# The first loads, the order of the queues, and two sums in the logits' banks: one change to a transformer block on one core

## The chip, the core and the metric

The kernel runs on one core of a Trainium2 chip. TensorE (PE) does the matmuls, VectorE (DVE), ScalarE (ACT) and GpSimd (POOL) the rest; SyncE (SP) issues nearly all DMAs. The metric is device time in microseconds (us); lower is better.

## The reference

One block on x of 2048 x 512 (bfloat16): a layernorm with scale and shift, sliding dilated attention (32 heads of 16, 8 keys at steps of 2) with a gated residual, a second such layernorm, and a gated FFN of width 1792 with a gated residual. Scales, shifts and gates are six blocks of 512 from one vector.

```python
mod = (silu(c) @ w_mod).reshape(c.shape[0], 6, 1, -1)
sa, ca, ga, sb, cb, gb = mod[:, 0..5]
h = layernorm(x) * (1 + ca) + sa
qkv = h @ wqkv                               # 32 heads of 16
idx = pos[:, None] - 2 * arange(8)           # masked where negative
logits = einsum('bhsd,bhswd->bhsw', q, k[idx]) * scale
x = x + ga * (einsum('bhsw,bhswd->bhsd', softmax(logits), v[idx]) @ wo)
h = layernorm(x) * (1 + cb) + sb
x = x + gb * ((gelu(h @ w_gate) * (h @ w_up)) @ w_down)
```

## The kernel before, in words

The 2048 rows go in four groups (0 to 3) of 512. For each group: layernorm statistics (`norm`, on DVE; `norm_act`, on ACT for some chunks), the normalised xn, a transpose, scale and shift into hT, then q, k, v (`qkv`, or for group 0 `qkv0_threads` in halves of 256 rows). The logits of 8 keys are products on DVE (`pq`, 128x4096 each, four a group), which PE sums over the 16 elements of a head by a 0/1 matrix M (`logits_mm`, LTp, in 32-row tiles of the array); softmax runs on DVE and ACT. The probabilities go through DRAM (`pt_dma`, escr to PT), v goes through DRAM too (`vload`: one store vscr, four loads V4 a group, V4 having one buffer). `pv` multiplies them on DVE (four a group), `pv_mm` sums them on PE into o_ps, again in 32-row tiles, `pv_ev` copies o_ps to oT on ACT, `x1_mm` projects with wo. Then the second layernorm, and the FFN (`ffn_mm`): 14 pairs of g_ps and u_ps, gelu and a copy on ACT, a product on DVE, then y_ps.

The modulation blocks 0 and 1 (shift and scale of the first layernorm) come from `cols` early on: w_mod columns as stationary operand, scT as a one-column moving operand. Blocks 2 to 5 come from `mods_g` (gR_ps) and go through DRAM (`gload`: a store and a load, gscr). `warmup` runs dummy matmuls on zeros while PE has no data.

PSUM is split into pools: "mm" with four buffers of one bank, "att" with two, "lg" with one buffer of two banks, which holds a group's logits LTp until its softmax is done.

Nothing is scheduled at run time by data. Every piece of work is an `Op` with its engine and the names it comes after, yielded by threads; `ORDER` is a written-out list of thread numbers, and `Issuer.run` takes the next operation of each thread named. That list fixes, on each engine, the order of its instructions, and on SP the order in which DMAs are issued. An engine works strictly in that order; between engines semaphores hold. Some thread numbers: 2 to 4 the first loads, 5 x's group 1, 6 and 7 wqkv's k and v, 11 w_mod blocks 2 to 4, 12 the FFN's weights, 29 the warm-ups, 36 hT of group 0 on DVE, 141 two dummy exponentials (`exp_table`); from 37 on, 26 threads for each group.

Of the kernel before, what the change touches and what calls it, by code (L numbers as in the profile page):

```python
# [106 lines left out]
def kernel(  # L107
# [90 lines left out]
    def warmup(cold, n):  # L198
        yield Op("DVE", 0.25, lambda: nc.vector.memset(gB[:], 0.0), fire="warm")
        for k in range(n):  # L200
            def f(k=k):
                if k == 0:
                    B["warm"] = T("mm", [P, SG], F32, "warm_ps")
                nc.tensor.matmul(B["warm"][:], lhsT=gB[:, 0:P], rhs=gB[:], start=True, stop=True)
            yield Op("PE", 0.427 if k < cold else 0.216, f, after=["warm"], take=[SL["mm"]] if k == 0 else [],
                     give=[SL["mm"]] if k == n - 1 else [], fire="warmed" if k == n - 1 else None)

    def loads():
# [20 lines left out]
        def ldwm01(k0, k1):  # L229
            def f():  # L230
                if "wm01" not in B:
                    B["wm01"] = T("prod", [P, 4, 2 * D], BF16, "wm01")
                nc.sync.dma_start(out=B["wm01"][:, k0:k1, :],  # L233
                                  in_=w_mod[k0 * P:k1 * P, 0:2 * D].rearrange("(t p) n -> p t n", p=P))
            return f
# [4 lines left out]
        def mb(n):  # L240
            return n / 0.333
# [21 lines left out]
        def act_q():  # L263
            yield Op("ACT", 0.45, ldc, fire="c", lat=0.0, dma=True)

        def sp_q():
            yield Op("SP", 0.47, ldx(0, 0, 1), fire="x0.0", lat=1.0)
            yield Op("SP", 0.47, ldx(0, 1, 2), fire="x0.1", lat=1.0)
            yield Op("SP", 0.47, ldwm01(0, 2), take=[SL["prod"]], fire="wmA", lat=1.3)
            yield Op("SP", 0.47, ldwm01(2, 3), fire="wmB", lat=0.6)  # L270
            yield Op("SP", 0.47, ldwm01(3, 4), fire="wmC", lat=0.6)
# [4 lines left out]
        def wq0_q():  # L276
            for dt in DT0:
                yield Op("SP", 0.47, ld(wqkv[0][:, dt, :], wq_v[:, dt, 0:D]), fire=f"wqkv0.{dt}", lat=0.35)
# [9 lines left out]
        def ffn_q():  # L288
# [691 lines left out]
```

## Time and profile before

| | |
|---|---|
| timed runs, median of 3 | 236.65 us (236.33 to 236.87) |
| the profiled execution's own time | 235.67 us |
| its span in the profile | 233.9 us |
| granted TensorE clock | 1.0 throughout |
| busy: PE, DVE, ACT, POOL | 229.3, 168.3, 149.9, 28.0 us |
| HBM read, written | 22.78 MB, 5.31 MB |

Times of instructions count from the start of the span; what lies around the span (1.8 us) is in the execution's time. In a row of the timeline stand the start, the duration, engine, line, operation, output <- inputs, the number of instructions merged, and in brackets the idle time before them with what ended it. "SPq" is SP's queue, where an issue's duration is that of issuing, not of the transfer. A row of windows gives the stretch, its width, the busy time (and instructions) of PE, PE's weight loads, DVE, ACT and POOL, the granted clock, the DMA engines' share and GB/s. A row of waits gives who waited for whom, the sum, the times and the longest. A row of DMA issues ends with the KB of one and the us from issue to landing.

### The profile page before, as it was taken

The numbers are of one execution on the slowest core, as the hardware profiler recorded it, in microseconds if no ns is written. First come the engines' busy times: TensorE is split into PE (matmuls) and PEld (weight loads), VectorE is DVE, ScalarE is ACT, GpSimd is POOL, SyncE is SP. The second block draws the span as 40 slices with busy tenths as digits, with TensorE's granted clock in tenths as the row PEclk, the third lists the DMA queues.
The fourth block names the chain that finished last, engine by engine and source line by source line (L and its number), as shares of the span: only waits on it lengthen the run. The fifth ranks groups of instructions, "written<-read, shape, count | busy, mean of one in ns | idle before, by whom it ended". The sixth has DMA issues, their size and how long they took to land.

```text
span 233.9 us, 3721 instructions
## 1 busy us (share of the span) xinstructions
PE 229.3 (98%) x1409; PEld 110.7 (47%) x1409; DVE 168.3 (72%) x242; ACT 149.9 (64%) x281; POOL 28.0 (12%) x37
## 2 busy tenths in 40 slices
PE   7999999999999999999999999999999999999995
PEld 2698445444644444444434443444444444444443
DVE  5799999899999999999999999684222221222222
ACT  4899998796994658937469663155766703666400
POOL 4111323300200000100000089010000000000000
PEclk9999999999999999999999999999999999999999
DMA  6997698947989807045509420605000011000011
GB/s 197 373 357 177 200 259 255 266 137 264 406 268 210 331 3 207 1 92 144 197 3 287 111 84 3 135 2 132 3 0 1 0 45 48 0 0 0 3 45 45
DMA packets 31961, 30.95 MB, mean 132 GB/s; under 512 B 17096, under 2 KB 27336, under 8 KB 31944
## 3 DMA queue, kind: packets, MB, share of 16 engines
q1 hardware_dynamic: 31936, 30.72, 43.3%
q8 instruction: 11, 0.18, 0.3%
q14 instruction: 6, 0.05, 0.1%
q10 hardware_dynamic: 8, 0.00, 0.0%
HBM read 22.78 MB, written 5.31 MB: 120 GB/s over the span
## 4 chain that ended last, share of the span: by engine, by line
PE 94%; DMA 2%; DVE 1%; SPq 1%; issue 0%
PE g_ps L842 21%; PE u_ps L842 21%; PE y_ps L854 19%; PE qkv_ps L618 14%; PE x_ps L812 6%; PE qkv_ps L557 4%; PE o_ps L791 3%; PE LTp L702 3%; DMA x<-in_A_x_dram 2%; PE y_ps L865 1%; DVE st L418 1%; PE hTp L472 1%; SPq L233 1%; SPq L218 1%; PE gR_ps L367 1%
## 5 line engine op out<-in xcount | busy, mean ns | idle before, releaser
L842 PE MATMUL u_ps<-h,Wu 128*128 128x512 bf16 x224 | 57.6, 380 | 0.0
L842 PE MATMUL g_ps<-h,Wg 128*128 128x512 bf16 x224 | 57.5, 379 | 0.0
L874 ACT ACTIVATE gl<-g_ps 128x512 bf16<-128x512 f32 x56 | 33.6, 601 | 29.5 <-PE g_ps L842 24.1
L892 DVE TENSOR_TENSOR hht<-gl,ub 128x512 bf16<-128x512 bf16 x56 | 23.2, 420 | 37.3 <-ACT ub L881 37.3
L854 PE MATMUL y_ps<-Wd,hht 128*128 128x512 bf16 x210 | 46.7, 380 | 0.0
L881 ACT CAST ub<-u_ps 128x512 bf16<-128x512 f32 x56 | 32.9, 587 | 12.0 <-PE u_ps L842 11.9
L777 DVE TENSOR_TENSOR pv<-PT,V 128x4096 bf16<-128x4096 bf16 x16 | 36.1, 2290 | 0.6 <-issue 0.6
L685 DVE TENSOR_TENSOR pq<-qT,kT 128x4096 bf16<-128x4096 bf16 (+1 forms) x17 | 36.2, 2157 | 0.0
L842 PEld LDWEIGHTS <-Wg 128*128 128x128 bf16 x224 | 21.7, 98 | 27.1 <-issue 1.5
L842 PEld LDWEIGHTS <-Wu 128*128 128x128 bf16 x224 | 21.8, 98 | 26.8 <-issue 0.8
L618 PE MATMUL qkv_ps<-hT,wqkv 128*128 128x512 bf16 x144 | 32.5, 380 | 0.0
L854 PEld LDWEIGHTS <-hht 128*128 128x128 bf16 x210 | 20.4, 98 | 25.2 <-issue 0.8
L449 POOL TENSOR_TENSOR rstd<-rstd,neghalf 128x4 f32<-128x4 f32 (+1 forms) x9 | 18.8, 2094 | 100.2 <-DVE rstd L443 51.6
L618 PEld LDWEIGHTS <-wqkv 128*128 128x128 bf16 x144 | 16.0, 115 | 15.3 <-issue 1.9
L899 DVE TENSOR_TENSOR ot<-y_ps,x 128x512 bf16<-128x512 f32 x15 | 10.3, 686 | 16.8 <-PE y_ps L854 16.8
L802 ACT CAST oT<-o_ps 128x512 bf16<-128x512 f32 x16 | 8.8, 593 | 9.9 <-PE o_ps L791 9.9
L812 PE MATMUL x_ps<-woP,oT 128*128 128x512 bf16 x64 | 15.1, 380 | 0.0
L418 DVE BATCH_NORM_STATS2 st<-x 128x6 f32<-128x512 bf16 x19 | 12.4, 682 | 2.0 <-DMA x<-in_A_x_dram 1.7
L510 ACT ACTIVATE h<-h,modT,scl 128x512 bf16<-128x512 bf16 x12 | 8.8, 803 | 7.8 <-DMA h<-xn 7.8
L557 PE MATMUL qkv_ps<-hT,wqkv 128*128 128x256 bf16 x96 | 11.5, 273 | 0.4 <-DMA wqkv<-in_A_wqkv_dram 0.3
L821 DVE TENSOR_TENSOR x<-x_ps,x 128x512 bf16<-128x512 f32 x16 | 10.7, 685 | 0.8 <-PE x_ps L812 0.8
L557 PEld LDWEIGHTS <-wqkv 128*128 128x128 bf16 x96 | 10.2, 114 | 1.5 <-DMA wqkv<-in_A_wqkv_dram 0.8
(80 smaller groups left out, 196.7 us busy)
## 6 DMA issues: line engine op xcount, KB each, us to landing
V<-vscr SPq DMA_DIRECT2D x16, 526.0 KB, 4.6
wm<-in_w_mod_dram SPq DMA_DIRECT2D x5, 512.0 KB, 6.5
vscr<-vT SPq DMA_DIRECT2D x4, 528.0 KB, 4.4
out_dram<-ot SPq DMA_DIRECT2D x15, 128.0 KB, 1.7
Wg<-in_B_w_gate_dram SPq DMA_DIRECT2D x4, 448.0 KB, 6.4
Wu<-in_B_w_up_dram SPq DMA_DIRECT2D x4, 448.0 KB, 10.1
x<-in_A_x_dram SPq DMA_DIRECT2D x3, 512.0 KB, 8.0
Wd<-in_B_w_down_dram SPq DMA_DIRECT2D x3, 512.0 KB, 8.1
```

The source lines that it names most:

```text
L418: nc.vector.bn_stats(out=k["st", c4][:], in_=src()[:, c4, :])
L449: nc.gpsimd.tensor_tensor(out=k["rstd"][:, a:b], in0=k["rstd"][:, a:b], in1=neghalf[:, a:b], op=ALU.pow)
L557: nc.tensor.matmul(B["qu", h, blk, u][:, jj, :], lhsT=wqkv[blk][:, dt, 2 * u + jj::4], rhs=B["hT", 0][:, 2 * h:2 * h + 2, dt, :], start=st ...
L618: nc.tensor.matmul(ps[:], lhsT=wqkv[blk][:, dt, j::4], rhs=B["hT", sg][:, :, dt, :], start=(dt == 0), stop=(dt == DT - 1))
L685: nc.vector.tensor_tensor(out=B["pq", sg, j][:, :, c0:c1], in0=_ap(B["qT", sg][:, j, c0:c1], [[0, W], [1, c1 - c0]]), in1=_ap(kT[:, j, sg ...
L777: nc.vector.tensor_tensor(out=t[:], in0=_ap(B["PT", sg][:, 0, :], [[SG, 2], [0, 4], [1, SG]]), in1=_ap(v[:, j, 0, :], [[8, 2], [VR, 4], [1 ...
L812: nc.tensor.matmul(ps[:], lhsT=B["oT", sg][:, j, c4 * P:(c4 + 1) * P], rhs=woP[:, j, :], start=(j == 0), stop=(j == 3))
L842: nc.tensor.matmul(ps[:], lhsT=Wt[:, dt, ft * P:(ft + 1) * P], rhs=B["h2T", sg][:, :, dt, :], start=(dt == 0), stop=(dt == DT - 1))
L854: nc.tensor.matmul(ps[:], lhsT=B["hh", sg, ft][:, c4 * P:(c4 + 1) * P], rhs=B["Wd", ft // 4][:, ft % 4, :], start=(ft == 0), stop=(ft == F ...
L874: nc.scalar.activation(out=gl[:], in_=B["g", sg, ft][:], func=ACT.Gelu_apprx_tanh)
L881: nc.scalar.copy(out=ub[:], in_=B["u", sg, ft][:])
L892: nc.vector.tensor_tensor(out=hh[:], in0=B["gl", sg, ft][:], in1=B["ub", sg, ft][:], op=ALU.mult)
```

## The change

- x's first group, four chunks of 128 rows, comes in two loads of two chunks (before: 1, 1, 2). w_mod's scale block goes in one load on ACT's queue; its shift block in two on SP's (before: both blocks together in three loads on SP). The scale gets its own PSUM tile, evicted by itself.
- q's columns of wqkv come in two loads (before four), k's in two (before one).
- k of group 0's first half runs block by block of the contraction, as q does, instead of unit by unit.
- One warm-up matmul fewer; the warm-ups write an "lg" buffer instead of an "mm" one, and q no longer waits for the last of them.
- For groups 2 and 3 (`LGO`) the third and fourth sum of `pv_mm` go to one "lg" buffer instead of two "att" ones.
- ORDER is new.

```diff
+            yield Op("ACT", 0.5, ldwm01(1, 0, 4, nc.scalar), take=[SL["prod"]], fire="wmS", lat=1.4, dma=True)
 ...
-            yield Op("SP", 0.47, ldx(0, 0, 1), fire="x0.0", lat=1.0)
-            yield Op("SP", 0.47, ldx(0, 1, 2), fire="x0.1", lat=1.0)
-            yield Op("SP", 0.47, ldwm01(0, 2), take=[SL["prod"]], fire="wmA", lat=1.3)
-            yield Op("SP", 0.47, ldwm01(2, 3), fire="wmB", lat=0.6)
-            yield Op("SP", 0.47, ldwm01(3, 4), fire="wmC", lat=0.6)
+            yield Op("SP", 0.47, ldx(0, 0, 2), fire="x0.0", lat=1.0)
+            yield Op("SP", 0.47, ldwm01(0, 0, 2, nc.sync), after=["wmS"], fire="wmA", lat=1.3)
+            yield Op("SP", 0.47, ldwm01(0, 2, 4, nc.sync), fire="wmB", lat=0.6)
 ...
-            for dt in DT0:
-                yield Op("SP", 0.47, ld(wqkv[0][:, dt, :], wq_v[:, dt, 0:D]), fire=f"wqkv0.{dt}", lat=0.35)
+            for dt in (2, 0):
+                yield Op("SP", 0.47, ld(wqkv[0][:, dt:dt + 2, :], wq_v[:, dt:dt + 2, 0:D]), fire=f"wqkv0.{dt}", lat=0.7)
+        def wq1_q():
+            for n in range(2):
+                yield Op("SP", 0.47, ld(wqkv[1][:, 2 * n:2 * n + 2, :], wq_v[:, 2 * n:2 * n + 2, D:2 * D]), fire=f"wqkv1.{n}", lat=0.7)
 ...
+                B["mp", b] = T("mm", [P, 4], F32, "modT_ps")
 ...
-        mm = [chain(fine(0, 0, (0, 1), DT0), unit(0, 1, 0), unit(0, 1, 1)), ...
+        mm = [chain(fine(0, 0, (0, 1), DT0), fine(0, 1, (0, 1), range(DT))), ...
 ...
+    LGO = (2, 3)
 ...
+                    if sg in LGO and j > 1:
+                        if j == 2:
+                            B["oL", sg] = T("lg", [P, W, P], F32, "o2_ps")
+                        o_ps = B["oL", sg][:, 4 * j - 8:4 * j - 4, :].rearrange("p w s -> p (w s)")
 ...
-    pl.spawn(warmup(10, 18))
+    pl.spawn(warmup(8, 17))
```

What the new ORDER list makes of SP's queue, read off with the threads' operations (x1 is x's group 1, V4.1.0 the first load of V of group 1, vst2 the store of v of group 2, wmN a block of w_mod, gst4 and gld4 the store and load of modulation block 4, est and pt the store and loads of the probabilities, tdma a transposing DMA):

```
before: x0 (3 loads) wmA wmB wmC x1 q (4 loads) k x2 wm2 v wo0 x3 wo1 wo2 wo3 wm3 wm4 gst2 vst0 ...
        V4.0.3 gld2 vst2 Wg.0 gst4 V4.1.0 Wg.1 Wg.2 gld4 Wg.3 Wu.0 Wu.1 Wu.2 Wu.3 wm5 Wd0 est1 V4.1.1 pt1 ...
after:  x0 (2 loads) wmA wmB q (2 loads) x1 k (2 loads) x2 v Wg.0 wo0 wm2 wo1 x3 wm3 wo2 wm4 wo3 gst2 vst0 ...
        V4.0.3 gld2 V4.1.0 vst2 Wg.1 gst4 V4.1.1 Wg.2 gld4 Wg.3 Wu.0 Wu.1 Wu.2 Wu.3 wm5 est1 pt1 ...
```

On DVE the same operations stand before the second layernorm of group 0 as before; hT's second half and the statistics of groups 1 to 3 change places among them. On PE the FFN's beginning is g, u, g, u in both; sums in 32-row tiles interrupt the FFNs at these places (LT logits, o the sums of pv, gR a modulation block; the first digit is the group):

```
before: u0.4|LT2.0-2 o1.0|g0.5  g0.9|o1.1 o1.2 gR5 LT2.3 o1.3|u0.9  u1.0|LT3.0-3|g1.1
        u1.4|o2.0 o2.1|g1.5  g1.5|o2.2 o2.3|u1.5  y1.0.0|o3.0 o3.1|y1.0.1  y1.1.0|o3.2 o3.3|y1.1.1
after:  g0.5|LT2.0-2 o1.0|u0.5  u0.9|o1.1 LT2.3 o1.2 gR5 o1.3|g0.10  u1.0|LT3.0-3|g1.1
        g1.5|o2.0 o2.1|u1.5  u1.9|o2.2 o2.3|g1.10  y1.1.1|o3.0-3|y1.2.0
```

On ACT the dummy exponentials stood in the head; in the new order the first stands before the second layernorm's sums of group 0, the second between the copy of u_ps 0 and the gelu of g_ps 1 of group 1's FFN, and that group's softmax exponential (of group 3's logits) before the copy of u_ps 3.

More of the change, by code (lines that the diff above doesn't have):

```diff
@@ L202, in f @@
                 if k == 0:
[L203 to L206, printed above, removed]
+                    B["warm"] = T("lg", [P, W, P], F32, "warm_ps")
+                nc.tensor.matmul(B["warm"][:, 0:4, :], lhsT=gB[:, 0:P], rhs=gB[:], start=True, stop=True)
+            yield Op("PE", 0.427 if k < cold else 0.216, f, after=["warm"], take=[SL["lg"]] if k == 0 else [],
+                     give=[SL["lg"]] if k == n - 1 else [], fire="warmed" if k == n - 1 else f"w{k}")
     def loads():
@@ L227, in ldwm, with ldwm01 @@
             return f
-        def ldwm01(k0, k1):
+        def ldwm01(b, k0, k1, q):
             def f():
                 if "wm01" not in B:
-                    B["wm01"] = T("prod", [P, 4, 2 * D], BF16, "wm01")
-                nc.sync.dma_start(out=B["wm01"][:, k0:k1, :],
-                                  in_=w_mod[k0 * P:k1 * P, 0:2 * D].rearrange("(t p) n -> p t n", p=P))
+                    B["wm01"] = T("prod", [P, 2, 4, D], BF16, "wm01")
+                q.dma_start(out=B["wm01"][:, b, k0:k1, :],
+                            in_=w_mod[k0 * P:k1 * P, b * D:(b + 1) * D].rearrange("(t p) n -> p t n", p=P))
             return f
@@ L294, in ffn_q, with cols @@
                 yield Op("SP", 0.65, ldwd(b), fire=f"Wd{b}", lat=mb(0.5 if b < 3 else 0.25), after=[f"qp.{g}.{blk}.3" for g in range(1, NSG) for blk in range(3)]
-                         + [f"qu.{h}.{blk}.{u}" for h in range(2) for blk in range(3) for u in range(2) if h + blk + u])
-        return (act_q(), sp_q(), xb_q(), wq0_q(), one(0.55, ldx(1), "x1", mb(0.5)), one(0.55, ldq(1), "wqkv1", mb(0.5)),
+                         + [f"qu.{h}.{blk}.{u}" for h in range(2) for blk in range(3) for u in range(2) if u or h or blk == 2])
+        return (act_q(), sp_q(), xb_q(), wq0_q(), one(0.55, ldx(1), "x1", mb(0.5)), wq1_q(),
                 one(0.55, ldq(2), "wqkv2", mb(0.5)), one(0.55, ldx(2), "x2", mb(0.5)), wo_q(),
                 one(0.55, ldx(3), "x3", mb(0.5)), wm_q(), ffn_q())
-    def cols(k0, k1):
+    def cols(b, k0, k1):
         def f():
             if k0 == 0:
-                B["mp"] = T("mm", [P, 8], F32, "modT_ps")
+                B["mp", b] = T("mm", [P, 4], F32, "modT_ps")
             for kt in range(k0, k1):
-                for ch in range(8):
-                    nc.tensor.matmul(B["mp"][:, ch:ch + 1], lhsT=B["wm01"][:, kt, ch * P:(ch + 1) * P],
-                                     rhs=scT[:, kt:kt + 1], start=(kt == 0 and ch == 0), stop=(kt == 3 and ch == 7))
+                for ch in range(4):
+                    nc.tensor.matmul(B["mp", b][:, ch:ch + 1], lhsT=B["wm01"][:, b, kt, ch * P:(ch + 1) * P],
+                                     rhs=scT[:, kt:kt + 1], start=(kt == 0 and ch == 0), stop=(kt == 3 and ch == 3))
         return f
@@ L344, in mods_mm @@
     def mods_mm():
-        yield Op("PE", 0.55, cols(0, 2), after=["wmA", "scT"], take=[SL["mm"]], fire="mpA")
-        yield Op("PE", 0.28, cols(2, 3), after=["wmB"], fire="mpB")
-        yield Op("PE", 0.28, cols(3, 4), after=["wmC"], give=[SL["prod"]], fire="mpC")
+        yield Op("PE", 0.55, cols(1, 0, 4), after=["wmS", "scT"], take=[SL["mm"]], fire="mpS")
+        yield Op("PE", 0.28, cols(0, 0, 2), after=["wmA"], take=[SL["mm"]], fire="mpA")
+        yield Op("PE", 0.28, cols(0, 2, 4), after=["wmB"], give=[SL["prod"]], fire="mpB")
     def mods_sc():
-        yield Op("ACT", 0.12, lambda: nc.scalar.add(out=scl[:, 0:4], in_=B["mp"][:, 4:8], add=1.0), after=["mpC"],
-                 fire="mod1")
+        yield Op("ACT", 0.12, lambda: nc.scalar.add(out=scl[:, 0:4], in_=B["mp", 1][:], add=1.0), after=["mpS"],
+                 give=[SL["mm"]], fire="mod1")
     def mods_sh():
-        yield Op("DVE", 0.12, lambda: nc.vector.tensor_copy(out=modT[:, 0:4], in_=B["mp"][:, 0:4]), after=["mpC"],
+        yield Op("DVE", 0.12, lambda: nc.vector.tensor_copy(out=modT[:, 0:4], in_=B["mp", 0][:]), after=["mpB"],
                  give=[SL["mm"]], fire="mod0")
@@ L535, in x_ready @@
     def x_ready(sg):
-        return lambda c4: [f"x0.{min(c4, 2)}"] if sg == 0 else [f"x{sg}"]
+        return lambda c4: [f"x0.{c4 // 2 * 2}"] if sg == 0 else [f"x{sg}"]
     def ln1(sg, a=0, b=4):
@@ L560, in wq0 @@
     def wq0(blk, dt):
-        return f"wqkv0.{dt}" if blk == 0 else f"wqkv{blk}"
+        return f"wqkv0.{dt // 2 * 2}" if blk == 0 else f"wqkv1.{dt // 2}" if blk == 1 else "wqkv2"
     def unit(h, blk, u):
@@ L575, in f @@
                     unit_mm(h, blk, u, dt, n == 0, n == 3)
-            yield Op("PE", 0.22 * len(us), f, after=[f"LN1.0.h{dt}.{h}", wq0(blk, dt)] + ["warmed"],
-                     take=[SL["mm"]] * len(us) if n == 0 else [], fire=f"qu.{h}.{blk}.{us[-1]}" if n == 3 else f"quf.{h}.{n}")
+            yield Op("PE", 0.22 * len(us), f, after=[f"LN1.0.h{dt}.{h}", wq0(blk, dt)] ,
+                     take=[SL["mm"]] * len(us) if n == 0 else [], fire=f"qu.{h}.{blk}.{us[-1]}" if n == 3 else f"quf.{h}.{blk}.{n}")
     def unit_ev(h, blk, u):
@@ L590, in g @@
                 nc.scalar.copy(out=B["vT", 0][:, o:o + 2, VH + h * 256:VH + h * 256 + 256], in_=ps[:])
-        yield Op("ACT", 0.485, g, after=[f"qu.{h}.{blk}.{1 if (h, blk) == (0, 0) else u}"] + (["vz.0"] if blk == 2 else []),
+        yield Op("ACT", 0.485, g, after=[f"qu.{h}.{blk}.{1 if h == 0 and blk < 2 else u}"] + (["vz.0"] if blk == 2 else []),
                  take=[SL["q"]] if (h, blk, u) == (0, 0, 0) else [], give=[SL["mm"]], fire=f"qe.{h}.{blk}.{u}")
@@ L602, in qkv0_threads @@
         v1 = [(1, 2, 0), (1, 2, 1)]
-        mm = [chain(fine(0, 0, (0, 1), DT0), unit(0, 1, 0), unit(0, 1, 1)), chain(*[unit(*a) for a in v0]),
+        mm = [chain(fine(0, 0, (0, 1), DT0), fine(0, 1, (0, 1), range(DT))), chain(*[unit(*a) for a in v0]),
               chain(fine(1, 0, (0,), DT1), *[unit(*a) for a in q1[1:]], *[unit(*a) for a in v1])]
@@ L786, in f @@
                 for j in range(j0, j0 + n):
-                    o_ps = T("att", [P, SG], F32, "o_ps")
+                    if sg in LGO and j > 1:
+                        if j == 2:
+                            B["oL", sg] = T("lg", [P, W, P], F32, "o2_ps")
+                        o_ps = B["oL", sg][:, 4 * j - 8:4 * j - 4, :].rearrange("p w s -> p (w s)")
+                    else:
+                        o_ps = T("att", [P, SG], F32, "o_ps")[:]
                     B["o", sg, j] = o_ps
@@ L792, in f @@
                                              start=(t == 0), stop=(t == 1), tile_position=(0, H * i))
-            yield Op("PE", 0.44 * n, f, quad=True, after=[f"pv.{sg}.{j0 + n - 1}", "consts"], take=[SL["att"]] * n, give=[SL["prod"]] * n,
+            yield Op("PE", 0.44 * n, f, quad=True, after=[f"pv.{sg}.{j0 + n - 1}", "consts"], take=[SL["att"]] * n if sg not in LGO or j0 < 2 else [SL["lg"]] if j0 == 2 else [], give=[SL["prod"]] * n,
                      fire=f"o.{sg}.{j0 + n - 1}")
@@ L801, in f @@
                     B["oT", sg] = T("ot4", [P, 4, SG], BF16, "oT")
-                nc.scalar.copy(out=B["oT", sg][:, j, :], in_=B["o", sg, j][:])
-            yield Op("ACT", 0.485, f, after=[f"o.{sg}.{min(b + n - 1 for b, n in heads(GV[sg]).items() if b + n > j)}"], take=[SL["ot4"]] if j == 0 else [], give=[SL["att"]],
+                nc.scalar.copy(out=B["oT", sg][:, j, :], in_=B["o", sg, j])
+            yield Op("ACT", 0.485, f, after=[f"o.{sg}.{3 if sg in LGO and j > 1 else min(b + n - 1 for b, n in heads(GV[sg]).items() if b + n > j)}"], take=[SL["ot4"]] if j == 0 else [], give=[SL["att"]] if sg not in LGO or j < 2 else [SL["lg"]] if j == 3 else [],
                      fire=f"oT.{sg}.{j}")
```

72 rows, old and new, of the table ORDER are left out of this document.

## The prediction

> **What bounds the kernel now.** I read the first part of the page (busy time by engine), then the waits of PE, then where PE's unbroken stretch begins and what feeds it there.
>
> ```profile
> PE 229.3 (98%) x1409; PEld 110.7 (47%) x1409; DVE 168.3 (72%) x242; ACT 149.9 (64%) x281; POOL 28.0 (12%) x37
> PE qkv_ps L557 <- DMA wqkv<-in_A_wqkv_dram: 0.3, 1, 0.3
> ```
>
> PE is busy for 98% of the span, and the row of its waits that falls last is the 0.3 us at L557, early on. So the end moves only in three ways: the point from which PE is fed without a break, a new wait behind that point, or PE's own work. PE alone doesn't settle the first of these. The windows of all engines, two stretches before the FFN and one from its start, show a second full engine:
>
> ```profile
> 14.00:41.60 27.60, 27.60 (x244) 17.53 (x242) 26.75 (x34) 26.67 (x60) 6.97 (x7) 1.00 0.84 237
> 41.70:61.80 20.10, 20.10 (x136) 9.38 (x135) 19.92 (x23) 15.93 (x32) 3.31 (x4) 1.00 0.76 255
> 65.00:231.00 166.00, 166.00 (x911) 74.48 (x909) 108.50 (x153) 94.26 (x164) 13.28 (x3) 1.00 0.28 82
> ```
>
> The third number after the span is DVE's: 26.75 of 27.6, then 19.92 of 20.1. Until about 62 us DVE is as full as PE; from 65 us DVE has 57 us to spare in 166. The two meet at group 0's second layernorm, in the timelines of DVE and of PE:
>
> ```profile
> 60.45 0.74 DVE L458 TENSOR_SCALAR xn<-x,sums,rstd 128x512 bf16<-128x512 bf16 x2
> 61.10 0.73 DVE L458 TENSOR_SCALAR xn<-x,mv,rstd 128x512 bf16<-128x512 bf16 x2
> ```
> ```profile
> 61.54 1.08 PE L472 MATMUL hTp<-ident,xn 128*128 128x128 bf16 x16
> 62.45 2.75 PE L618 MATMUL qkv_ps<-hT,wqkv 128*128 128x512 bf16 x12
> 65.05 1.03 PE L842 MATMUL g_ps<-h,Wg 128*128 128x512 bf16 x4
> 65.91 0.60 PE L842 MATMUL u_ps<-h,Wu 128*128 128x512 bf16 x2
> ```
>
> PE starts the transposes of xn at 61.54 and DVE finishes the last xn at 61.10+0.73 = 61.83: no slack. So the FFN's first matmul, 65.05, hangs on DVE as much as on PE, and all that comes after it is PE work without a gap (166.00 of 166).
>
> **The change, part by part.**
>
> *The head (loads, scale block, warm-ups).* q's weights pass x's second group on SP's queue, and that group of 512 KB falls behind them.
>
> ```profile
> 9.77 0.63 PE L557 MATMUL qkv_ps<-hT,wqkv 128*128 128x256 bf16 x4 [0.30 <-DMA wqkv<-in_A_wqkv_dram]
> ```
> ```profile
> 2.50:3.00 0.50, 0.50 (x3) 0.23 (x2) 0.08 (x1) 0.46 (x2) 0.14 (x3) 1.00 0.83 242
> 3.00:3.50 0.50, 0.50 (x3) 0.23 (x2) 0.50 (x1) 0.00 (x0) 0.00 (x0) 1.00 0.22 70
> 10.00:11.00 1.00, 1.00 (x15) 0.99 (x14) 1.00 (x4) 0.97 (x5) 0.00 (x0) 1.00 1.09 386
> ```
> ```profile
> 8.58 0.73 DVE L526 TENSOR_SCALAR hT<-hTp,scl,modT 128x256 bf16<-128x256 bf16 x2
> 9.45 1.29 DVE L418 BATCH_NORM_STATS2 st<-x 128x6 f32<-128x512 bf16 x2
> ...
> 11.79 1.04 DVE L526 TENSOR_SCALAR hT<-hTp,scl,modT 128x256 bf16<-128x256 bf16 x3
> 13.00 0.41 DVE L458 TENSOR_SCALAR xn<-x,mv,rstd 128x512 bf16<-128x512 bf16 x1 [0.17 <-POOL rstd L449]
> ```
> ```profile
> DVE ssum L735 <- ACT LTp L730: 0.2, 1, 0.2
> ```
>
> The last number of a window is GB/s. The full rate is 386; between 2.5 and 3.5 us the loads ran at 242 and 70, since small loads are issued one after another. Larger first loads and a second issuing engine fill that hole: (386-242)x0.5 + (386-70)x0.5 = 230 KB, 0.6 us. For q's weights 512/386 = 1.3 us of x leave the way; their matmuls then wait for hT. Its start, 8.58, hangs on the same 1.5 MB of x and w_mod as now and on the same chain on ScalarE, so I leave it; the first hT is ready at 8.58+0.4, and PE starts at about 9.1, not 9.77: 0.7 us ahead (between 0 and 1.3). For x's second group 1.3 us are added and 0.6 taken: it lands at about 10.15, not 9.45 (between 9.6 and 10.6). From these statistics to the xn at 13.00 DVE takes 3.55 us now; one of the three hT (1.04/3 = 0.35) moves ahead of the load and the 0.17 wait is covered, so 3.0 us, and DVE is at the same point at 13.15: 0.15 late. The softmax's sum waits 0.2 for the exponential now, and the two dummy exponentials (0.2 each) leave ScalarE's queue ahead of it; I count 0.05 back of the 0.2. DVE at 61.8 is then 0.1 late (between 0.5 early and 0.6 late), and PE's 0.7 lead ends in waiting for it: worth nothing. The scale's own PSUM tile, one warm-up less and k's first half taken by contraction blocks keep PE's matmuls in number and cost nothing, as PE waits for loads or for DVE either way; without that cover a warm-up is 0.2.
>
> A rule of the Trainium skill bears on the second queue: "DMA: Bandwidth & Descriptors", section "Issuing engines are not separate DMA queues", says that loads started by ScalarE and by SP run on the same 16 DMA engines and interleave, so that a second issuer saves issue time alone. No row of this run shows two large loads side by side. By that rule x's own tiles share the rate with the scale block, which is the third rival below.
>
> *The order of SP's queue.* In the new order the first load of V of group 1 stands ahead of the store of V of group 2, of w_gate's second block and of the store of modulation row 4; now it stands behind them. The timeline of SP, its waits between 43 and 52 us, and the windows of the DMA:
>
> ```profile
> 43.42 1.11 SPq L656 DMA_DIRECT2D vscr<-vT  x1
> 44.58 0.43 SPq L210 DMA_DIRECT2D Wg<-in_B_w_gate_dram  x1
> 45.06 0.55 SPq L312 DMA_DIRECT2D gscr<-gR  x1
> 50.65 0.55 SPq L664 DMA_DIRECT2D V<-vscr  x1
> 51.24 1.06 SPq L210 DMA_DIRECT2D Wg<-in_B_w_gate_dram  x2
> 52.34 0.43 SPq L319 DMA_DIRECT2D modc<-gscr  x1
> 52.82 0.96 SPq L210 DMA_DIRECT2D Wg<-in_B_w_gate_dram  x1
> 53.83 2.34 SPq L210 DMA_DIRECT2D Wu<-in_B_w_up_dram  x4
> ```
> ```profile
> SPq L664 <- DVE pv L777: 4.1, 1, 4.1
> ```
> ```profile
> 34.00:35.00 1.00, 1.00 (x6) 0.39 (x4) 0.96 (x2) 1.00 (x3) 0.32 (x1) 1.00 1.05 401
> 49.00:50.00 1.00, 1.00 (x6) 0.57 (x5) 1.00 (x1) 1.00 (x3) 0.00 (x0) 1.00 0.00 0
> 52.00:53.00 1.00, 1.00 (x6) 0.48 (x5) 1.00 (x1) 0.62 (x2) 0.00 (x0) 1.00 1.03 257
> ```
> ```profile
> Wu<-in_B_w_up_dram SPq DMA_DIRECT2D x1, 448.0 KB, 10.1
> ```
>
> The load of V has one buffer and waits at the head of SP's queue until DVE's last pv of group 0 frees it, at 50.6. Now the store and one weight block go out before that wait, at 43.42 and 44.58, while the DMA would otherwise idle (0 GB/s at 49). Afterwards they stand behind it. That weight block, w_gate's first, goes out far earlier in exchange, ahead of x's last group and two blocks of w_mod: it pushes these by 448/386 = 1.2 us, of which the filled hole gives 0.6 back, and their readers stand later in the new order too, so I count nothing (0.6 on DVE if that cover fails). The store of V (528 KB) does add, and so does V's second load (526 KB), which follows w_up now and in the new order precedes w_gate's last two blocks and all of w_up. Queued behind the waiting instruction are thus the store, three blocks of w_gate, the modulation row's store and load, and w_up's four blocks; PE waits for the last of these in the FFN's first up-projection.
> Its price: the last block of w_up, whose row stands last, is issued at 55.5 and lands 10.1 later, 65.6, fifteen us after V's load is issued. The two added transfers take (528+526)/401 = 2.6 us at the best rate of such transfers (34 to 35 us), and at the 257 GB/s of the window in which this load of V runs, 4.1. I take 2.7, near the first, because a store of V and a load of V were both in flight in that window: the block lands at 68.35. PE's fourth matmul of u_ps, the first to read it, would start at 65.91+3x0.216 = 66.56 (0.216 is a quarter of the 0.86 between 65.05 and 65.91). So PE stands still for 1.8 us. Ends: no block is late, 0; or 4.1 us added and the first matmul already waiting for all of w_up, 65.6+4.1-65.91 = 3.8. In PE's order nothing can pass it. Modulation row 4, whose store and load now also come later, feeds the scale of the second layernorm; by the same sum it lands about 62, just when ScalarE reads it (62.4), so nothing, or up to 0.5 inside the same wait.
>
> *The order of PE, the logits' banks.* A group of sums on 32 rows among other matmuls costs a change of mode each time, in the chain that ended last:
>
> ```profile
> 118.86 0.86 PE u_ps L842 x4
> 119.72 0.98 PE o_ps L791 x16
> 120.70 0.97 PE g_ps L842 x4
> ```
>
> Sixteen such matmuls are four full ones, 0.86, but took 0.98, and the projection behind took 0.97: 0.22 for a group. From the FFN's start there are 7 groups now and 6 in the new order (group 3's four sums stand together, which the two borrowed buffers allow): 0.22 gained. More than that the buffers can't bring, as the third window has no PE gap for them to close; were the logits' banks still in use, a group's last two sums would wait for group 3's softmax, which the new order puts before them on DVE.
>
> *The dummy exponentials.* The second now stands between two gelus of group 1's FFN, so a table goes to exp and back.
>
> ```profile
> 98.78 1.28 ACT L730 ACT_TABLE_LOAD   x1
> 100.07 1.01 ACT L730 ACTIVATE LTp<-LTp 128x1024 f32<-128x1024 f32 x1
> ```
> ```profile
> 113.72 0.60 ACT L874 ACTIVATE gl<-g_ps 128x512 bf16<-128x512 f32 x1 [2.23 <-PE g_ps L842]
> ```
>
> Two loads of 1.28 and a dummy of 0.2 make 2.8; ScalarE idles 2.23 at that place now, so the next gelu comes 0.55 late, and PE has four PSUM buffers, 4x0.86 = 3.4 us, before it would notice: nothing, at most 0.5. The Trainium skill ("ScalarE: Activation LUTs", section "What ACT_TABLE_LOAD costs") puts a switch at 2.66 us with its drain, which by its figure would make the gelu 3.3 late and eat that cover; the trace doesn't agree, as the load took 1.28 and the exponential began at 100.07, 1.29 after the load.
>
> *Sum.* +1.8 (w_up late) +0.1 (DVE) -0.2 (one group less) = +1.7 us. On the profiled execution's 235.67 that is 237.4. That execution stands 1.0 below the median of the timed runs, 236.65, and the forecast is for such a median: 238.3.
>
> **The rivals.**
> *Faster, 13%.* w_up isn't late and DVE is early. Mechanism: the loads' hole closes further than the queue lengthens, x's second group lands by 9.6, DVE gains 0.55-0.15 = 0.4 and the covered 0.2 of the softmax's wait: -0.6, and -0.2 for the group: 235.9. It decides if the last block of w_up lands before 66.5, 0.9 us later than now. For it speaks the full engine, DVE, which any head start would help; against it that 1.05 MB are added ahead of a block that has 0.9 us to spare.
> *No change, 12%.* The store goes out in time all the same (the wait isn't at the queue's head, or V's buffer is freed sooner), DVE comes out 0.1 late: 236.65+0.1-0.2 = 236.55. Against it: the 4.1 us wait is in the trace.
> *DVE late, 7%.* The scale block takes half the rate from x's first group, whose second load then lands up to 0.7 later (256/386), the mods follow, and DVE is 0.6 late, with w_up in time: +0.6: 237.2. The hole before 3.5 us speaks against so much. The Trainium skill's section on issuing engines, cited above, speaks for it.
> *Tables as well, 5%.* w_up late, and the switches stall PE 0.5 or more: 239.
>
> **How the numbers follow.** The forecast, w_up late, has 63%; its own range goes from a tail of 0.5 us (the block's last packets catch up a us) to 3: 237.1 to 239.6. With DVE late and the tables, slower by over 0.2% (0.47 us, about what a measurement of this kernel can tell from no change) has 75%, within it 12%, faster 13%. The range from 236.3 to 239.6 takes in the forecast's, DVE late, and most of no change, and leaves out the faster case.
>
> **What would show it.** In the changed profile SP's V load sits at about 50.6 with the vT store, three w_gate blocks and w_up behind; a DMA wait of 1 to 3 us appears at PE's first u_ps (L842), which had none. PE starts L557 near 9.1, DVE's first statistics of group 1 near 10.1, and xn of the second layernorm ends within 0.6 us of 61.8. Two more table loads appear, with no PE gap behind. If u_ps starts with no DMA wait, the forecast is wrong, and DVE's time at xn decides the sign.

## The result and the profile after

The changed kernel takes 239.03 us (median of 16 runs, 237.73 to 241.7) beside 236.70 for the kernel before on the same chip: a ratio of 1.0092, 95% interval 1.0069 to 1.0116. A second comparison, at another time, gave 238.34 and 1.0076 (1.0045 to 1.0106). The forecast was 238.3, slower, in a range from 236.3 to 239.6. An execution more than 1.5% above the fastest of its kernel is left out of every comparison here and below.

Two profiles of the changed kernel are read here, since its head differs from run to run: the first, of an execution of 240.71 us, and that of the second comparison, of 237.66 (before: 235.67). First the start of the page of the first, then PE's waits over 0.6 us:

```profile
span 239.0 us, 3718 instructions
PE 231.3 (97%) x1408; PEld 112.0 (47%) x1408; DVE 168.2 (70%) x242; ACT 153.2 (64%) x283; POOL 19.3 (8%) x37
```
```profile
PE u_ps L851 <- DMA Wu<-in_B_w_up_dram: 1.5, 3, 0.7
...
PE modT_ps L309 <- DMA wm<-in_w_mod_dram: 1.1, 1, 1.1
```

The wait for w_up, which the kernel before didn't have, is there, and a second one at the modulation matmuls (0.2 us before). In the second profile PE's timeline at the start of the FFN reads:

```profile
65.40 1.03 PE L851 MATMUL g_ps<-h,Wg 128*128 128x512 bf16 x4
66.26 0.59 PE L851 MATMUL u_ps<-h,Wu 128*128 128x512 bf16 x2
67.72 0.39 PE L851 MATMUL u_ps<-h,Wu 128*128 128x512 bf16 x1 [0.86 <-DMA Wu<-in_B_w_up_dram]
68.77 0.39 PE L851 MATMUL u_ps<-h,Wu 128*128 128x512 bf16 x1 [0.66 <-DMA Wu<-in_B_w_up_dram]
68.99 1.03 PE L851 MATMUL g_ps<-h,Wg 128*128 128x512 bf16 x4
```

From the first u_ps to the next g_ps it takes 68.99-66.26 = 2.73 us instead of 0.86: PE stands for 1.87. The two xn of the second layernorm that end last stand in DVE's timeline of the same profile:

```profile
61.34 0.73 DVE L461 TENSOR_SCALAR xn<-x,mv,rstd 128x512 bf16<-128x512 bf16 x2
```

They end at 62.07, against 61.83 before, and g_ps starts at 65.40 against 65.05. The second g_ps of the kernel before, and in the chains that ended last DVE's last instruction, in the kernel before and in the second profile:

```profile
66.77 1.03 PE L842 MATMUL g_ps<-h,Wg 128*128 128x512 bf16 x4
```
```profile
231.18 0.29 DVE ot L906
```
```profile
233.35 0.29 DVE ot L915
```

From the second g_ps to DVE's last instruction it is 233.35-68.99 = 164.36 against 231.18-66.77 = 164.41, and to the end of the span 235.9-68.99 = 166.9 against 233.9-66.77 = 167.1. So +0.35, +1.87 and -0.2 make +2.0, which is the difference of the two executions (237.66-235.67 = 1.99).

In the first profile the stall at the first u_ps is 2.04 us, and xn ends at 64.77, 2.9 late:

```profile
69.10 0.38 PE L851 MATMUL u_ps<-h,Wu 128*128 128x512 bf16 x1
...
72.00 1.03 PE L851 MATMUL g_ps<-h,Wg 128*128 128x512 bf16 x4
```
```profile
64.04 0.73 DVE L461 TENSOR_SCALAR xn<-x,mv,rstd 128x512 bf16<-128x512 bf16 x2
```

The late xn comes from the head, which the same profile's timeline of PE and its windows show:

```profile
8.19 1.02 PE L309 MATMUL modT_ps<-scT,wm 128*128 128x1 bf16 x32 [1.11 <-DMA wm<-in_w_mod_dram]
```
```profile
8.00:9.00 1.00, 0.81 (x29) 0.80 (x30) 0.09 (x1) 0.99 (x2) 0.75 (x2) 1.00 1.01 354
9.00:10.00 1.00, 1.00 (x17) 0.79 (x16) 0.54 (x3) 0.43 (x3) 0.00 (x0) 0.69 1.09 385
10.00:11.00 1.00, 1.00 (x5) 0.54 (x4) 1.00 (x3) 0.74 (x2) 0.00 (x0) 0.50 1.07 378
11.00:12.00 1.00, 1.00 (x10) 0.88 (x9) 0.00 (x0) 0.00 (x0) 0.00 (x0) 0.50 1.08 378
12.00:13.00 1.00, 1.00 (x9) 0.83 (x8) 0.56 (x2) 0.88 (x2) 0.00 (x0) 0.60 1.07 378
```

The modulation's matmuls start at 8.19 instead of 6.78 in the second profile, PE has stood for 1.1 us ahead of them, and the granted clock (the number ahead of the DMA's share) then falls to 0.50 while PE is busy. q, which DVE's next steps wait for, runs at half speed. If the clock of a window is made of stretches at 0.50 and at 1.00, the four windows hold 0.62+1+1+0.80 = 3.4 us at 0.50 (0.69 stands for 0.62 us, 0.60 for 0.80). Of the 15 executions in the comparison, five had a mean clock of 0.993 like this one and average 240.5; the ten at full clock average 238.4.

### The profile page after: what moved, and what is told of

Read it like the earlier page. It is cut to its first block, busy times and chain, and to the rows that moved or that the text cites. A ratio compares the mean times of both kernels' runs of the same rounds, so it can differ in the third digit from the quotient of the medians.

```text
span 239.0 us, 3718 instructions
## 1 busy us (share of the span) xinstructions
PE 231.3 (97%) x1408; PEld 112.0 (47%) x1408; DVE 168.2 (70%) x242; ACT 153.2 (64%) x283; POOL 19.3 (8%) x37
## 4 chain that ended last, share of the span: by engine, by line
PE 78%; DMA 9%; ACT 4%; POOL 3%; DVE 3%; SPq 1%; issue 0%; ACTq 0%
PE u_ps L851 20%; PE g_ps L851 20%; PE y_ps L863 19%; PE qkv_ps L621 5%; PE x_ps L821 4%; DMA Wu<-in_B_w_up_dram 3%; POOL rstd L452 3%; PE o_ps L800 3%; DMA wm<-in_w_mod_dram 3%; DMA gscr<-gR 2%; PE LTp L706 2%; PE qkv_ps L560 2%; PE y_ps L874 1%; ACT hT L513 1%; SPq L210 1%; DVE xn L461 1%
## 5 line engine op out<-in xcount | busy, mean ns | idle before, releaser
L621 PE MATMUL qkv_ps<-hT,wqkv 128*128 128x512 bf16 x144 | 33.1, 380 | 1.1 <-ACT hT L513 0.6
L452 POOL TENSOR_TENSOR rstd<-rstd,neghalf 128x4 f32<-128x4 f32 (+1 forms) x9 | 15.3, 1700 | 114.9 <-DVE rstd L441 60.8
L621 PEld LDWEIGHTS <-wqkv 128*128 128x128 bf16 x144 | 16.0, 114 | 16.7 <-issue 3.6
L560 PEld LDWEIGHTS <-wqkv 128*128 128x128 bf16 x96 | 10.7, 117 | 0.8 <-issue 0.5
```

The costliest lines, as they stand in the source:

```text
L452: nc.gpsimd.tensor_tensor(out=k["rstd"][:, a:b], in0=k["rstd"][:, a:b], in1=neghalf[:, a:b], op=ALU.pow)
L560: nc.tensor.matmul(B["qu", h, blk, u][:, jj, :], lhsT=wqkv[blk][:, dt, 2 * u + jj::4], rhs=B["hT", 0][:, 2 * h:2 * h + 2, dt, :], start=st ...
L621: nc.tensor.matmul(ps[:], lhsT=wqkv[blk][:, dt, j::4], rhs=B["hT", sg][:, :, dt, :], start=(dt == 0), stop=(dt == DT - 1))
```

## The experiments

Where an edit is one of order, the diff gives the order on that engine by names; V.0 and V.1 are the first two loads of V of group 1, "row 4" is modulation row 4. Every ratio is to the kernel before, on the same chip.

**SP's order mended.**

```diff
 SP:
-V.0, store of V 2, Wg.1, row 4 store, V.1, Wg.2, row 4 load, Wg.3, Wu.0-3
+store of V 2, Wg.1, row 4 store, V.0, Wg.2, row 4 load, Wg.3, Wu.0-3, ..., V.1
```

> The changed kernel, with V's first load of group 1 put back behind the store of V of group 2, w_gate's second block and modulation row 4's store on SP's queue, and V's second load put back behind w_up. Theory (two separate losses: a head that is late and a w_up that is late): PE's DMA wait for w_up at its first u_ps, 2.2 us from the gap in the changed profile, is gone, the head stays as late as it was (xn of the second layernorm ends between 62.5 and 65, PE idle before 8.2 us), and the time falls by 1.7 to 2.2 from the changed kernel's 239.0 to about 237. Rival 1 (the late w_up follows from the late head alone): the time is within 0.5 of the changed kernel. Rival 2 (the head costs nothing): the time is at or below the kernel before, 236.7.

Measured: 236.89 us, ratio 1.0005 (0.9983 to 1.0028). The wait for w_up is gone, and the whole measured loss is undone by SP's order alone: by the interval, the rest of the change together is worth between -0.4 and +0.7 us. Rival 1 fell. Between the theory (237) and rival 2 (at or below before) the time can't decide. In the profile xn was 1.5 late:

```profile
62.61 0.72 DVE L461 TENSOR_SCALAR xn<-x,mv,rstd 128x512 bf16<-128x512 bf16 x2
```

But this execution took 237.17 us, 0.3 above its median, and the profile before is of one that stands 1.0 below its own. That the medians agree while these two profiles differ by 1.5 means that the late xn here is in the main the spread between executions; a loss by the head in the median isn't shown.

**The scale block on SP**, and **both edits together**.

```diff
-yield Op("ACT", 0.5, ldwm01(1, 0, 4, nc.scalar), ...)
+yield Op("SP", 0.5, ldwm01(1, 0, 4, nc.sync), ...)   # behind x's two loads
```

> The changed kernel, with w_mod's scale block issued on SP behind x's first group (x, x, scale, shift, shift) instead of on ScalarE's queue. Theory (the second queue slows x and itself lands late, and PE's gap while it waits makes the clock fall): first statistics back at 2.9 to 3.4 us instead of 3.70, scale block landed by about 7.0 instead of 8.15, no gap of PE over 0.7 us ahead of modT_ps, granted clock 1.00 in every window up to 14 us, xn of the second layernorm within 0.6 us of 61.8 instead of 64.8, the w_up wait of about 2.2 us still there, the time 237.9 to 238.5. Rival (rows of 1 KB of the split w_mod loads, or the larger first load of x, make the head late, not the queue): the scale block is no sooner than 7.9 and the time stays near 239.

> Both edits together: the scale block issued on SP, and V's loads back in their old places on SP's queue. Theory (the two losses add and are all): 236.3, between 236.0 and 236.8, no DMA wait at the first u_ps, PE's work from the FFN's start 0 to 0.2 below the kernel before. If something else costs (tables, DVE's new order), it shows here as 237 or more, with the clock at 1.00.

Measured: 239.59 us, 1.0152 (1.0104 to 1.0199), and 237.53 us, 1.0032 (0.9998 to 1.0067). The theory fell. DVE's copy of the shift, the first thing that waits for all of w_mod's first two blocks, in the kernels with SP's order mended, first with the scale block on ScalarE's queue, then on SP:

```profile
8.91 0.16 DVE L357 COPY modT<-modT_ps 128x4 f32<-128x4 f32 x1 [1.89 <-PE modT_ps L309]
```
```profile
9.29 0.16 DVE L357 COPY modT<-modT_ps 128x4 f32<-128x4 f32 x1 [2.35 <-PE modT_ps L309]
```

With the block on SP the shift comes 0.4 later in this pair, about one issue (0.47); the shift's own loads are issued behind it. One pair of profiles would prove little, but the shift was ready (the copy's end) at 9.45 and 9.67 in the two kernels with the block on SP, and by 9.42 or sooner in all nine profiles with it on ScalarE's queue. So ScalarE's queue isn't what makes the head late. That the kernel with the block on SP alone is slower than the changed kernel itself fits the later shift in kind; all of it isn't explained.

**The kernel before with the changed order of SP around V.**

```diff
 SP:
-x3 ... store of V 2, Wg.0, row 4 store, V.0, Wg.1, Wg.2, row 4 load, Wg.3, Wu.0-3, ..., V.1
+Wg.0, x3 ... V.0, store of V 2, Wg.1, row 4 store, V.1, Wg.2, row 4 load, Wg.3, Wu.0-3
```

> The kernel before, with the changed kernel's order on SP's queue around V alone: w_gate's first block early, V's first load ahead of the store of V of group 2, w_gate's second block and modulation row 4's store, V's second load ahead of w_gate's last two blocks and w_up. Theory (the order of SP's queue by itself makes w_up late): head and DVE as in the kernel before (first xn of the second layernorm within 0.3 of 60.45), a DMA wait of 1.5 to 3 us at PE's first u_ps, the time 238.2 to 239.5 against 236.7. Rival (w_up has room and is late in the changed kernel only as its head is late): within 0.4 of the kernel before.

Measured: 240.26 us, 1.0154 (1.0112 to 1.0196). The order alone costs more than the whole change, but not at w_up: u_ps has no wait. In the chain that ended last stand:

```profile
63.17 0.23 POOL scl L325
63.40 1.01 POOL rstd L450
...
64.44 0.42 DVE xn L459
```

In the kernel before, GpSimd makes the scale of row 4 (`scl`) ahead of the power of the second layernorm (`rstd`), at 59.19 and 59.38. Row 4 now lands late, the power waits behind its scale, and DVE's xn waits 2.1 us for the power; xn ended at 65.82, 4.0 late. 2.0 of it are there by the last pv: among others, DVE waited 0.9 us for x of group 3, behind which w_gate's first block used to stand and ahead of which it now goes out (in the new order this reader stands later). By 65.82 w_up has landed. The changed kernel's order puts the power ahead of row 4's scale, and the same lateness shows at w_up instead. Both sizes expected were wrong in their place.

**Row 4's load behind w_up**, and **V's second load late**, each from the changed kernel.

```diff
 SP (row 4 last):
-V.1, Wg.2, row 4 load, Wg.3, Wu.0-3
+V.1, Wg.2, Wg.3, Wu.0-3, row 4 load
```
```diff
 SP (V.1 late):
-row 4 store, V.1, Wg.2, row 4 load, Wg.3, Wu.0-3
+row 4 store, Wg.2, row 4 load, Wg.3, Wu.0-3, ..., V.1
```

> The changed kernel with one load moved: modulation row 4 is read back behind w_gate's last block and all of w_up instead of ahead of them; V's loads stay in their new places. In the changed kernel SP's queue stands still for 2.5 to 3.3 us ahead of this load, since it waits until the store of the same row, issued 4.8 to 5.7 us earlier, has landed. Theory (the wait for the store's landing holds w_up back): w_up is issued about 3 us earlier, PE's DMA wait at the first u_ps falls from about 1.9 us to under 0.5, and the time falls by 1.2 to 1.9, to about 237.0 where the changed kernel is 238.6. Rival 1 (the two added transfers hold it back by their bytes, as the prediction's sum has it): the last block lands within 0.5 us of where it did, no change. Rival 2 (row 4 now late at ScalarE's modulated hT): a wait of 0.5 to 1 there, and as much of the gain lost.

> The changed kernel with V's second load of group 1 back behind w_up; V's first load stays ahead of the store of V. Theory of bytes (the prediction's sum): 526 KB less ahead of w_up, 526/401 = 1.3 us, so the wait at the first u_ps falls from about 1.9 to 0.6 us and the time by 1.0 to 1.3. Rival (SP's wait for the store of modulation row 4 sets when w_up is issued): the issues of w_up stay where they are, the wait falls by at most 0.5 us.

Why these two: in the second profile of the changed kernel SP's timeline and the chain that ended last show what the prediction hadn't costed.

```profile
51.05 0.53 SPq L667 DMA_DIRECT2D V<-vscr  x1
51.69 0.52 SPq L659 DMA_DIRECT2D vscr<-vT  x1
52.26 0.42 SPq L210 DMA_DIRECT2D Wg<-in_B_w_gate_dram  x1
52.78 1.10 SPq L315 DMA_DIRECT2D gscr<-gR  x1
53.93 0.53 SPq L667 DMA_DIRECT2D V<-vscr  x1
54.52 0.61 SPq L210 DMA_DIRECT2D Wg<-in_B_w_gate_dram  x1
57.63 0.38 SPq L322 DMA_DIRECT2D modc<-gscr  x1
58.05 0.50 SPq L210 DMA_DIRECT2D Wg<-in_B_w_gate_dram  x1
58.60 2.12 SPq L210 DMA_DIRECT2D Wu<-in_B_w_up_dram  x4
```
```profile
52.78 4.83 DMA gscr<-gR
...
60.02 8.70 DMA Wu<-in_B_w_up_dram
```

SP issues nothing from 55.1 to 57.6: row 4's load waits until its store has landed, 4.83 us after its issue, with V and w_gate in flight. w_up stands behind.

V.1 late: 238.29 us, 1.0063 (1.0041 to 1.0085). With 526 KB less ahead of w_up the standstill is no shorter (3.5 us, 55.5 to 59.0), and the DMA runs dry behind it; SP's timeline and a window:

```profile
55.08 0.43 SPq L210 DMA_DIRECT2D Wg<-in_B_w_gate_dram  x1
58.98 0.38 SPq L322 DMA_DIRECT2D modc<-gscr  x1
```
```profile
60.00:62.00 2.00, 2.00 (x11) 1.07 (x10) 1.97 (x7) 1.76 (x5) 1.15 (x2) 1.00 0.51 85
```

w_up's last block landed at 69.35, 17.3 us after the last pv of group 0 (52.06), against 68.72-51.02 = 17.7 in the changed kernel. So 1.3 us less of transfer (526 KB at 401 GB/s) bought 0.4: the rival holds.

Row 4 last: 244.45 us, 1.0317 (1.0282 to 1.0353). SP no longer stood still ahead of w_up, and issued it from 55.7 to 58.5 (with 1.2 us of waiting between the second block and the third, while the DMA moved 409 GB/s). Its last block landed 8.9 us after its issue, at 67.4, 16.4 after the last pv (50.98): 1.3 sooner than in the changed kernel. But row 4 then came far too late; GpSimd, ScalarE and PE in turn:

```profile
67.83 2.07 POOL L327 TENSOR_SCALAR scl<-modc 128x4 f32<-128x4 bf16 x1 [7.07 <-DMA modc<-gscr]
```
```profile
69.93 2.79 ACT L513 ACTIVATE h<-hTp,modT,scl 128x512 bf16<-128x512 bf16 x4 [7.09 <-POOL scl L327]
```
```profile
70.76 2.60 PE L851 MATMUL g_ps<-h,Wg 128*128 128x512 bf16 x4 [5.24 <-ACT h L513]
```

Rival 2, at many times the size expected: a load of 1 KB behind 2.2 MB is as late as these. The run also says how the 1.87 us divide. Counted from the last pv, the last block of w_up landed after 15.0 us in the kernel before (65.6-50.6), after 16.4 without SP's standstill, and after 17.7 in the changed kernel: 1.4 us are the queue's added bytes, 1.3 the wait for row 4's store. PE's fourth u_ps would want the block at 66.26+3x0.216 = 66.91, and without the standstill it comes at 67.4, so of PE's stall the bytes alone would leave 0.5 (an estimate, from different kernels).

**Warm-ups against the clock**, beside the changed kernel itself.

```diff
-pl.spawn(warmup(8, 17))
+pl.spawn(warmup(8, 22))     # five more, ahead of modT_ps
```

> The changed kernel itself, for comparison on the same chip. Expected 238.0 to 239.5, 0.9% over the kernel before; about a third of its executions at a mean clock of 0.993 instead of 1.00, and these some 2 us longer than the others, as in its first runs (six of sixteen, 239.6 to 241.0 against 237.7 to 239.5).

> The changed kernel with five more warm-up matmuls ahead of modT_ps (5x0.216 = 1.1 us, the length of the gap that PE showed there). Theory (the gap of 1.1 us is what makes the clock fall to a half for 3.4 us in a third of the executions): every execution at a mean clock of 1.00, the median 0.5 to 0.9 below the changed kernel's, near the 238.4 that its executions at full clock average. Rival 1 (the clock falls by chance, whatever PE does there): the same share at 0.993, the same median. Rival 2 (the warm-ups delay modT_ps when its load is early): 0.1 to 0.4 slower.

Measured: the changed kernel 238.34 us, with five more warm-ups 239.11, 1.012 (1.0075 to 1.0165). Two of its six executions fell to 0.993 all the same. In the profiled one PE had no gap ahead of modT_ps and the clock was 1.00 there; it fell at the wait for w_up. Windows 68 to 69 and 71 to 73:

```profile
68.00:69.00 1.00, 0.39 (x1) 0.10 (x1) 1.00 (x2) 0.98 (x2) 0.00 (x0) 1.00 0.97 365
...
71.00:72.00 1.00, 1.00 (x4) 0.30 (x2) 1.00 (x1) 0.33 (x1) 0.00 (x0) 0.50 0.09 34
72.00:73.00 1.00, 1.00 (x4) 0.34 (x3) 1.00 (x2) 0.59 (x1) 0.00 (x0) 0.50 0.00 0
```

So the theory fell: without the gap in the head the clock still falls. Of the kernels whose profile shows PE waiting a us or more at modT_ps, u_ps or g_ps, 25 of 88 executions were at 0.993 or less; of the three orders of DVE below, whose PE waits behind the first warm-up are all under 1 us, 2 of 34, and of the kernel before 8 of 67. But by kernel the share goes from none (SP's order mended, 0 of 12 with a gap of 1.1 in its profile; V's second load late, 0 of 9) to 5 of 6 (w_mod in whole rows, next) and 6 of 6 (row 4 last, where PE waits 5.2). A wait of a us or two goes with the fall, then, but isn't enough for it; what else decides isn't shown.

**w_mod in whole rows.**

```diff
-scale block on ACT, shift block on SP in two       (rows of 1 KB)
+both blocks together on SP, k 0-1 and k 2-3        (rows of 2 KB), SP's order mended
```

> The kernel with SP's order mended, and w_mod's first two column blocks loaded as in the kernel before, in rows of 2 KB, both blocks together, in two loads on SP behind x (no load on ScalarE's queue). Theory (rows of 1 KB and the split by columns make shift and scale late: the split load had shift ready at 8.9 to 9.5 us in four profiles, the kernel before at 8.2 to 8.7): shift is ready by 8.4, DVE's first statistics of group 1 start 0.5 to 0.9 earlier than the 11.4 of the kernel with SP's order alone, the time 0.3 to 0.8 below it. Rival (x's loads ahead, or the two blocks of q behind, set the time): shift no earlier than 8.8, no change of the time.

Measured: 239.23 us, 1.0133 (1.0091 to 1.0175). The shift was ready at 9.68, later still, and five of six executions were at 0.993 or 0.986, PE's waits for w_mod adding up to 1.9 us. The theory fell. What makes the head vary isn't settled: with the scale on ScalarE's queue the shift was ready between 7.8 and 9.4 in nine profiles, with no load changed ahead of it.

**DVE's order.** In every profile of the changed kernel one power of 128x4 on GpSimd takes 7.7 us. First the row before, then that with SP's order mended, with DVE's wait for it:

```profile
20.41 1.01 POOL L449 TENSOR_TENSOR rstd<-rstd,neghalf 128x4 f32<-128x4 f32 x1 [7.33 <-DVE rstd L443]
```
```profile
19.12 7.71 POOL L452 TENSOR_TENSOR rstd<-rstd,neghalf 128x4 f32<-128x4 f32 x1 [3.80 <-DVE rstd L446]
```
```profile
19.27 6.69 DVE L689 TENSOR_TENSOR pq<-qT,kT 128x4096 bf16<-128x4096 bf16 x3
26.87 0.74 DVE L461 TENSOR_SCALAR xn<-x,mv,rstd 128x512 bf16<-128x512 bf16 x2 [0.91 <-POOL rstd L452]
```

The kernel before had group 3's first statistics at 20.44, beside the power. Three edits, all with SP's order mended:

```diff
 early:  SP: Wg.0 back behind the store of V 2
-DVE: rstd 2, xn 1, pq, pq, pq, xn 2 ..., st 3
+DVE: rstd 2, st 3, xn 1, pq, pq, pq, xn 2 ...
 mid:    DVE: rstd 2, xn 1, pq, pq, st 3, pq, xn 2 ...
 both:   mid, and the first st of group 1 ahead of the hT that waits 0.5 for PE
```

> The kernel with SP's order mended (V's loads in their old places) and in addition w_gate's first block back behind the store of V of group 2, and on DVE the first statistics of group 3 back directly behind the rstd of group 2's layernorm, ahead of pq. Theory (GpSimd's power of 128x4 took 7.7 us in the changed kernel, against 1.01 before, as DVE ran three pq of 2.2 us beside it, and DVE then waited 0.9 us for it; x of group 3 lands later because w_gate's block stands ahead of it): the power takes 1.0 to 1.7 again, DVE's wait of 0.9 is gone, and the time is 0.5 to 1.0 below the kernel with SP's order alone, about 236.2 where that is 236.9. Rival 1 (DVE has that slack elsewhere): no change. Rival 2 (w_gate's blocks late at the FFN's first matmul): a wait at g_ps and 0.5 or more slower.

> The kernel with SP's order mended, and on DVE the first statistics of group 3 ahead of the last of group 0's four pq instead of behind group 2's xn. Theory (GpSimd gets nothing done beside pq and finishes its power of 128x4 beside the statistics; x of group 3 has landed by then, 20.7 to 23.2 us in the profiles): the power ends about 2.5 us earlier, DVE's wait of 0.9 us for it is gone, x's statistics wait for no DMA, and the time is 0.5 to 0.9 below the kernel with SP's order alone and below the kernel before: 236.0 to 236.4 where that is 236.9. Rival 1 (the 0.9 comes back at DVE's next wait): no change. Rival 2 (x of group 3 is late): a DMA wait at the statistics, slower.

> The same, and on DVE the first statistics of group 1 ahead of the modulated hT for which DVE waits 0.5 us at 10.5 us. Theory (DVE is full from there to the second layernorm, so a filled wait is worth its length): another 0.3 to 0.5 lower, about 235.8. Rival (x of group 1 lands later than 10.5 us): the statistics wait for the DMA, and PE's q waits for hT: 0.3 or more slower.

Measured: early 237.72 us, 1.0047 (1.0023 to 1.0070); mid 236.15, 0.9986 (0.9959 to 1.0013); both 236.39, 0.9986 (0.9963 to 1.0009). Early made the power 1.01 again, but x of group 3 wasn't there, and the wait came back longer:

```profile
19.82 0.69 DVE L421 BATCH_NORM_STATS2 st<-x 128x6 f32<-128x512 bf16 x1 [1.49 <-DMA x<-in_A_x_dram]
```

Mid brought the power down to 5.51, and the wait of 0.9 is gone:

```profile
18.00 5.51 POOL L452 TENSOR_TENSOR rstd<-rstd,neghalf 128x4 f32<-128x4 f32 x1 [3.71 <-DVE rstd L446]
```
```profile
22.56 0.69 DVE L421 BATCH_NORM_STATS2 st<-x 128x6 f32<-128x512 bf16 x1
```

From group 1's first statistics to the last xn DVE takes 51.4 us instead of 51.95: 0.55 of the 0.9. In the kernel with both, the statistics of group 1 waited 0.7 us for x, as the rival had it, and nothing more was gained. Mid has the lowest median of all kernels tried, but by the ratio it is level with both, and the interval of neither excludes the time of the kernel before.

## Why the prediction was right, point by point

- **w_up late, +1.8.** Right in place and size: 1.87 and 2.04 us in two profiles, and the undoing of SP's order took the whole loss back (1.0092 to 1.0005). Its working was wrong in part. The sum held the bytes added ahead of w_up alone, 2.7 us of lateness at the rates of the windows; the lateness was 2.7 indeed (17.7 against 15.0 us behind the last pv), but by the run with row 4 last the bytes made only 1.4 of it. The other 1.3 is a wait that the sum didn't have: it named row 4's store and load among what is queued, but costed them at their size, and the load waits for the landing of its own store and holds all of SP for 2.5 us in the second profile and 3.2 in the first. That bytes costed too high and a wait left out came to the same 2.7 is luck.
- **Row 4 lands about 62, nothing to 0.5.** Right here (GpSimd's scale at 61.1 in the second profile, ScalarE's reader at 62.8), though only since the new order on GpSimd puts the power first: on the old order the same lateness cost DVE 2.1 us. The prediction named ScalarE as the reader and missed GpSimd, whose queue was on the way.
- **DVE 0.1 late (0.5 early to 0.6 late).** 0.24 late in the second profile, 2.9 in the first, 1.5 with SP's order mended, each against one profile of the kernel before that was itself 1.0 below its median. In the median no loss is shown (1.0005 with SP's order mended), so the centre stands as far as is known; the range was too narrow, and its weak step is that hT's start "hangs on the same 1.5 MB of x and w_mod as now and on the same chain on ScalarE, so I leave it": the shift was ready at 7.8 to 9.4, in the kernel before at 8.3 and, with SP's order changed far behind it, at 8.8. DVE's statistics of group 1 started at 10.30 in the second profile (10.15 forecast) and at 12.77 in the first. The wait of the softmax's sum, 0.2, went as said; another came, 0.9 for GpSimd's power.
- **The warm-up less, "without that cover 0.2".** The term left the clock out: in the first profile PE's gap was 1.1 us and the clock at a half for 3.4 us behind it, and executions at that mean clock took 2.1 us more (240.5 against 238.4). That the missing warm-up brings this isn't shown: five more didn't make the kernel faster, and with SP's order mended the same gap left the clock at 1.00.
- **PE starts q at 9.1.** 8.89 in the second profile. That it is worth nothing fits, but not because DVE alone sets the pace: DVE's third hT, at 9.97, waited 0.50 for the transposes that PE makes behind q.
- **One group of sums less, -0.2.** Mis-sized: to DVE's last instruction 0.05 less. The 0.2 to the end of the span is a difference of spans read to 0.1 us, with the last store in it.
- **Two table loads more, no gap of PE.** ScalarE has 283 instructions for 281, and PE has no DMA or ScalarE wait over 0.1 us behind the first u_ps.
- **The rivals.** Faster and no change needed w_up in time: it wasn't. DVE late by the scale block on ScalarE's queue: DVE was late at times, but with the block on SP the shift came later still. Tables as well: no gap of PE showed.

## What to carry to other kernels

Cost a moved DMA by what its engine's queue waits for, not by its bytes alone: a small load that waits for a store's landing stops everything that is issued behind it, and the store lands late when large transfers are ahead of it. Follow each late operand to every reader in every queue, for an order elsewhere decides whether it costs 0 or 2 us. Where the head of a kernel is a race of loads, give its term the spread of several profiles, not of one, and see where the profiled execution stands among the timed ones before a difference to it is called a loss.

## What the runs showed of the hardware

- The clock fell to 0.50 for some 3.4 us behind waits of PE of 1.1 us (first profile, 7.1 to 8.2) and of 0.4, 0.7 and 0.7 within 3 us (the kernel with more warm-ups), in 25 of 88 executions of kernels with such a wait in their profile, and not in others with the same gap. The Trainium skill ("TensorE: Matmul & The Clock Gate", section "Why this matters for your kernels") puts the limit at gaps of about 3 us; here shorter ones did it.
- GpSimd's power, 1.01 us by itself, took 7.71 beside three products of DVE in a row and 5.51 when statistics came behind two: it ended 0.87 us after DVE had left the products (26.83 against 25.96; 23.51 against 22.65). The Trainium skill ("SBUF — State Buffer", section "Who interferes with whom") says that a DVE instruction with two SBUF inputs and a GpSimd instruction that reads SBUF exclude each other; the trace agrees, and in it GpSimd didn't get in between two of them.
- A store of 1 KB took 4.83 us to land while V and w_gate were in flight, and a load of 1 KB issued at 58.9 us behind 2.2 MB was used at 67.8.
